# A Fourier filter and a gated layer on one core: the sums and third low parts of the combination move from GpSimd to VectorE

## The chip, the core and the metric

One core of a Trainium2 chip runs the whole program. The metric is the device time of one execution in microseconds (us). Five engines work side by side: TensorE (PE, with its weight loads as PEld), VectorE (DVE), ScalarE (ACT), GpSimd (POOL), and SyncE (SP), which here only issues transfers.

## What is computed

The reference, cut to what matters (numpy; 8 batches of 3008 rows of 256):

```
X = rfft(x, axis=1);  Xr, Xi = X.real, X.imag
Yr = Xr @ w_r - Xi @ w_i + b_r
Yi = Xr @ w_i + Xi @ w_r + b_i
Yr, Yi = soft threshold of each by 0.01
y = irfft(Yr + 1j * Yi, n=3008, axis=1)
h = y @ w_in            # 256 -> 2048
out = (h * cos(h)) @ w_out   # 2048 -> 256
```

All is float32. A float32 product is made on TensorE from two parts of each operand, a rounded high part and the low part that is left, in three matmuls (high by high, low by high, high by low).

## The kernel before

**Two streams.** The main stream is the layer: 8 batches of 6 tiles of 512 rows (the last of 448), and for each tile 16 steps `f`, one per 128 columns of `w_in`: 768 steps. Beside it, while batch `b` goes through the layer, the Fourier filter of batch `b+1` is made. `fourier` (a generator) gives out its work piece by piece, and each step of the layer pulls some of it by written-out costs. A scheduler then sets the order on each engine from its own estimates of time; on the chip each engine takes its instructions in that order and waits for semaphores.

**A step of the layer** (`moe_step`, `second`) is a chain through four engines. TensorE makes `ph` in six matmuls (L939 to L941, 128x512 each); ScalarE rounds `ph` over two pi to whole turns (L949); VectorE subtracts (L950); ScalarE takes the sine (L952); VectorE multiplies by `ph` (L953); ScalarE casts the product to its high part `gh` (L954); then the low part `gl` is formed, by GpSimd (`rest_pool`, L329) where `f` mod 4 is 0 or 2, by VectorE (`rest`, L332) otherwise. TensorE's second product reads `gh` in four matmuls (L921, L922) and `gl` in two (L925). It trails the first product by three steps (`SKEW`), so that the chain has time.

**The combination** (`combine`) belongs to the Fourier filter. For a batch it runs four times (`q` = 0 to 3), for batches 1 to 7: 28 times. It takes the real part `z[:, 0]` and the imaginary part `z[:, 1]` of the spectrum, each in two halves `v`, and forms three operands for the product with the weights: the real part, the imaginary part and their sum. Each is split in high and low:

- first operand: ScalarE casts `Xh` (L602), VectorE subtracts `Xl` (`rest`, L332), for both halves;
- the sum is written in place over the real part (L609), on GpSimd, so it waits for the first operand's low part; beside it ScalarE casts the imaginary part (L610) and VectorE forms its low part (L332);
- third operand: ScalarE casts the sum (L617), GpSimd forms its low part (`rest_pool`, L329).

`wmix` then multiplies the operands by the weights into `pw`: L668 and L669 read high parts, L670 low parts, and the first of its products reads the third operand (the sum). Its results pass through VectorE (L679 to L694) and a `fold` on GpSimd (L707 to L719) into block transposes on VectorE (L724, L725).

Of the kernel before, what the change touches and what calls it, by code (L numbers as in the profile page):

```python
# [19 lines left out]
ALU = mybir.AluOpType  # L20
# [158 lines left out]
def tile_body(ctx: ExitStack, tc, x, w_r, w_i, b_r, b_i, w_in, w_out,  # L179
              c_fq, c_sig, c_f3, c_ff, c_if, c_iw, c_sgn, out):  # L180
    nc = tc.nc
# [139 lines left out]
    def floor():  # L321

        ctx = ExitStack()
        for ins in steps[-2] if len(steps) > 1 else ():
            ctx.enter_context(tc.issue_after(ins.ins))
        return ctx

    def rest_pool(lo, x, hi):
        return nc.gpsimd.tensor_tensor(out=lo, in0=x, in1=hi.bitcast(F32), op=ALU.subtract)  # L329

    def rest(lo, x, hi):
        return nc.vector.tensor_tensor(out=lo, in0=x, in1=hi.bitcast(F32), op=ALU.subtract)  # L332
# [199 lines left out]
    def stage_b(b):  # L532
# [58 lines left out]
        def combine(q):  # L591

            z = Z.pop(q).rearrange("p (v z g m k) -> p g v z m k", v=2, z=2, g=2, m=8)[..., :24]
            xyh = wk.tile([128, 2304], F32R, tag="Xh", name="Xh", bufs=1)
            xyl = wk.tile([128, 2304], F32R, tag="Xl", name="Xl", bufs=1)
            hi, lo = ([m[:, 768 * r:768 * r + 768].rearrange("p (v m z k) -> p v z m k", v=2, m=8, z=2) for r in range(3)]
                      for m in (xyh, xyl))
            X[q] = tuple([[m[:, 768 * r:768 * r + 768].rearrange("p (v c x) -> p c v x", v=2, c=2)[:, c] for c in range(2)]
                          for r in range(3)] for m in (xyh, xyl))
            for v in range(2):  # L600
                with floor():
                    nc.scalar.copy(hi[0][:, v], z[:, 0, v])  # L602
                yield 0.8
                with floor():
                    rest(lo[0][:, v], z[:, 0, v], hi[0][:, v])
                yield 0.9
            for v in range(2):
                with floor():
                    nc.gpsimd.tensor_tensor(out=z[:, 0, v], in0=z[:, 0, v], in1=z[:, 1, v], op=ALU.add)  # L609
                    nc.scalar.copy(hi[1][:, v], z[:, 1, v])  # L610
                yield 0.9
                with floor():
                    rest(lo[1][:, v], z[:, 1, v], hi[1][:, v])
                yield 1.2
            for v in range(2):
                with floor():
                    nc.scalar.copy(hi[2][:, v], z[:, 0, v])  # L617
                yield 0.8
                with floor():
                    rest_pool(lo[2][:, v], z[:, 0, v], hi[2][:, v])  # L620
                yield 0.9

        X, ST = {}, {}
# [187 lines left out]
        def first():  # L811
# [7 lines left out]
            yield from inverse(3)  # L819

        return SimpleNamespace(first=first, load=load, forward=forward, combine=combine, wmix=wmix, inverse=inverse)

    stages = {}
# [289 lines left out]
```

## Time and profile before

| what | value |
|---|---|
| median of 3 runs | 2598.45 us (2598.3 to 2601.07) |
| the profiled execution: its own time | 2597.48 us |
| the profiled execution: span from first to last instruction | 2595.7 us |
| TensorE matmuls busy | 99% of the span |
| VectorE, ScalarE, GpSimd busy | 75%, 63%, 38% |
| mean granted clock of TensorE | 0.997 |

How to read it: the busy share of an engine is an average over the program. Matmul ends are modelled, so a busy row overlaps the next one; what TensorE loses is read from its idle times in the list of waits and in the rows in order of time. A row in order of time gives its start, its length, the engine, the line, what it writes and reads with the shape, how many neighbours it merges, and in brackets the idle time of the engine before it with what ended it.

### The profile page before, as it was taken

The numbers are of one execution on the slowest core, as the hardware profiler recorded it, in microseconds if no ns is written. First come the engines' busy times: TensorE is split into PE (matmuls) and PEld (weight loads), VectorE is DVE, ScalarE is ACT, GpSimd is POOL, SyncE is SP. The second block draws the span as 40 slices with busy tenths as digits, with TensorE's granted clock in tenths as the row PEclk, the third lists the DMA queues.
The fourth block names the chain that finished last, engine by engine and source line by source line (L and its number), as shares of the span: only waits on it lengthen the run. The fifth ranks groups of instructions, "written<-read, shape, count | busy, mean of one in ns | idle before, by whom it ended". The sixth has DMA issues, their size and how long they took to land.

```text
span 2595.7 us, 42932 instructions
## 1 busy us (share of the span) xinstructions
PE 2558.0 (99%) x15961; PEld 2064.4 (80%) x15961; DVE 1938.6 (75%) x3089; ACT 1628.6 (63%) x3003; POOL 977.6 (38%) x946
## 2 busy tenths in 40 slices
PE   9899999999999999999999999999999999999999
PEld 7477778877788778887788877887778888888888
DVE  5887876877778777787777877777776778766665
ACT  5665556665665666666666666666666666666666
POOL 2035452544324453344523454234432333322222
PEclk9999999999999999999999999999999999999999
DMA  7536434354334443254432644235433334210000
GB/s 236 175 107 166 130 110 117 106 143 130 112 87 118 133 132 106 81 151 129 138 88 85 166 130 119 90 101 141 130 101 102 89 106 121 60 49 21 17 25 16
DMA packets 172953, 283.11 MB, mean 109 GB/s; under 512 B 15608, under 2 KB 114200, under 8 KB 169160
## 3 DMA queue, kind: packets, MB, share of 16 engines
q1 hardware_dynamic: 161896, 243.78, 33.5%
q0 software_dynamic: 10112, 35.53, 4.3%
q8 instruction: 126, 2.06, 0.3%
q10 hardware_dynamic: 736, 1.05, 0.1%
q14 instruction: 83, 0.68, 0.1%
HBM read 149.76 MB, written 130.55 MB: 108 GB/s over the span
## 4 chain that ended last, share of the span: by engine, by line
PE 84%; DVE 8%; ACT 3%; DMA 2%; issue 2%; POOL 0%; SPq 0%; DVEq 0%; ACTq 0%; POOLq 0%
PE ph L939 12%; PE po L921 12%; PE ph L940 12%; PE ph L941 11%; PE po L925 11%; PE po L922 11%; PE pw L668 2%; PE pw L669 2%; PE pw L670 2%; DVE u L953 2%; PE pb L381 1%; PE pc L381 1%; DVE u L950 1%; DVE Xl L332 1%; ACT gh L954 1%
## 5 line engine op out<-in xcount | busy, mean ns | idle before, releaser
L329 POOL TENSOR_TENSOR gl<-u,gh 128x512 fp32r<-128x512 f32 (+1 forms) x384 | 501.4, 1306 | 1115.8 <-ACT gh L954 928.4
L952 ACT ACTIVATE u<-u 128x512 f32<-128x512 f32 (+1 forms) x768 | 478.0, 623 | 389.1 <-DVE u L950 388.2
L953 DVE TENSOR_TENSOR u<-ph,u 128x512 f32<-128x512 f32 (+1 forms) x768 | 518.0, 675 | 237.8 <-ACT u L952 226.6
L950 DVE SCALAR_TENSOR_TENSOR u<-ph,u 128x512 f32<-128x512 f32 (+1 forms) x768 | 513.4, 671 | 236.5 <-ACT u L949 235.6
L954 ACT CAST gh<-u 128x512 fp32r<-128x512 f32 (+1 forms) x768 | 467.8, 609 | 250.3 <-DVE u L953 247.9
L921 PE MATMUL po<-gh,wout 128*128 128x512 f32 (+1 forms) x1536 | 600.0, 391 | 15.9 <-ACT gh L954 15.8
L949 ACT ACTIVATE u<-ph 128x512 int32<-128x512 f32 (+1 forms) x768 | 447.6, 586 | 259.2 <-PE ph L941 250.5
L939 PE MATMUL ph<-xTh,win 128*128 128x512 f32 (+1 forms) x1536 | 603.4, 393 | 1.8 <-ACT xTh L901 1.6
L940 PE MATMUL ph<-xTl,win 128*128 128x512 f32 (+1 forms) x1536 | 595.9, 388 | 0.1
L941 PE MATMUL ph<-xTh,win 128*128 128x512 f32 (+1 forms) x1536 | 594.9, 387 | 0.0
L922 PE MATMUL po<-gh,wout 128*128 128x512 f32 (+1 forms) x1536 | 593.8, 387 | 0.0
L925 PE MATMUL po<-gl,wout 128*128 128x512 f32 (+1 forms) x1536 | 476.1, 387 | 0.0
L939 PEld LDWEIGHTS ph<-xTh,win 128*128 128x128 f32 x1536 | 289.3, 188 | 90.6 <-issue 18.4
L332 DVE TENSOR_TENSOR gl<-u,gh 128x512 fp32r<-128x512 f32 (+1 forms) x384 | 297.2, 774 | 79.8 <-ACT gh L954 71.6
L921 PEld LDWEIGHTS po<-gh,wout 128*128 128x128 f32 x1536 | 288.2, 188 | 86.1 <-ACT gh L954 26.2
L925 PEld LDWEIGHTS po<-gl,wout 128*128 128x128 f32 x1536 | 287.2, 188 | 60.1 <-issue 4.9
L941 PEld LDWEIGHTS ph<-xTh,win 128*128 128x128 f32 x1536 | 289.5, 188 | 56.9
L940 PEld LDWEIGHTS ph<-xTl,win 128*128 128x128 f32 x1536 | 289.5, 188 | 51.0 <-DVE xTl L902 0.6
L922 PEld LDWEIGHTS po<-gh,wout 128*128 128x128 f32 x1536 | 288.5, 188 | 50.8
L332 DVE TENSOR_TENSOR Xl<-z,Xh 128x384 fp32r<-128x384 f32 x112 | 108.4, 996 | 11.9 <-ACT Xh L602 8.9
L668 PE MATMUL pw<-Xh,wf 128*128 128x384 f32 x336 | 115.0, 342 | 2.2 <-ACT Xh L617 2.2
L717 POOL TENSOR_TENSOR odd<-st 128x184 f32<-128x184 f32 (+1 forms) x112 | 68.2, 611 | 125.5 <-DVE st L694 117.2
(123 smaller groups left out, 2444.0 us busy)
## 6 DMA issues: line engine op xcount, KB each, us to landing
scrF<-at SPq DMA_DIRECT2D x28, 1024.0 KB
z<-scrF SPq DMA_DIRECT2D x112, 256.0 KB
scrT<-tr SPq DMA_DIRECT2D x56, 512.0 KB
y<-scrT SPq DMA_DIRECT2D x112, 256.0 KB
bt<-scr SPq DMA_DIRECT2D x94, 256.0 KB
scr<-ao SPq DMA_DIRECT2D x84, 256.0 KB
scr<-bo SPq DMA_DIRECT2D x224, 96.0 KB
out_dram<-ob SPq DMA_DIRECT2D x80, 256.0 KB
```

Of the source, the lines that this page charges most:

```text
L329: return nc.gpsimd.tensor_tensor(out=lo, in0=x, in1=hi.bitcast(F32), op=ALU.subtract)
L921: mm(po[e][:, :n], wo[0][:, 0, f, es], gh[:, :n], start=f == 0, stop=False)
L922: mm(po[e][:, :n], wo[0][:, 1, f, es], gh[:, :n], start=False, stop=False)
L925: mm(po[e][:, :n], wo[0][:, 0, f, es], gl[:, :n], start=False, stop=f == NFC - 1)
L939: mm(h, win[:, 0, c, fs], th[:, c, :n], start=c == 0, stop=False)
L940: mm(h, win[:, 0, c, fs], tl[:, c, :n], start=False, stop=False)
L941: ins = mm(h, win[:, 1, c, fs], th[:, c, :n], start=False, stop=c == 1)
L949: nc.scalar.activation(k[:, :n], h, AF.Identity, bias=0.25, scale=1.0 / TWO_PI)
L950: nc.vector.scalar_tensor_tensor(out=u[:, :n], in0=h, scalar=1.0 / TWO_PI, in1=k[:, :n], op0=ALU.mult, op1=ALU.subtract)
L952: nc.scalar.activation(u[:, :n], u[:, :n], AF.Sin, bias=HALF_PI, scale=TWO_PI)
L953: product = nc.vector.tensor_tensor(out=u[:, :n], in0=h, in1=u[:, :n], op=ALU.mult)
L954: step = [nc.scalar.copy(gh[:, :n], u[:, :n])]
```

## The change

In `combine`, the two sums (L609) are formed by VectorE, and so are the two low parts of the third operand (L620, `rest` in place of `rest_pool`). Nothing else in the text of the program differs.

```
             for v in range(2):
                 with floor():
-                    nc.gpsimd.tensor_tensor(out=z[:, 0, v], in0=z[:, 0, v], in1=z[:, 1, v], op=ALU.add)
+                    nc.vector.tensor_tensor(out=z[:, 0, v], in0=z[:, 0, v], in1=z[:, 1, v], op=ALU.add)
                     nc.scalar.copy(hi[1][:, v], z[:, 1, v])
...
                 with floor():
-                    rest_pool(lo[2][:, v], z[:, 0, v], hi[2][:, v])
+                    rest(lo[2][:, v], z[:, 0, v], hi[2][:, v])
                 yield 0.9
```

The order in which the scheduler puts the instructions moves with it. Three places follow; all are of batch 4's filter, made while batch 3 goes through the layer, and the filters of batches 2 to 6 repeat them.

VectorE, `q` = 2 (tile 2 of the layer's batch 3; `u_12170`, `u_12216`, `u_12247` are its steps `f` = 2, 3 and 4; `z_11744` and `Xl_12206` are the combination's). Before:

```order
L953 TENSOR_TENSOR u_12170<-ph_12163,u_12170 128x512
L950 SCALAR_TENSOR_TENSOR u_12216<-ph_12209,u_12216 128x512
L332 TENSOR_TENSOR Xl_12206<-z_11744,Xh_12205 128x2x8x24 x2
L950 SCALAR_TENSOR_TENSOR u_12247<-ph_12240,u_12247 128x512
L953 TENSOR_TENSOR u_12216<-ph_12209,u_12216 128x512
```

and with the change:

```order
L953 TENSOR_TENSOR u_12170<-ph_12163,u_12170 128x512
L609 TENSOR_TENSOR z_11744<-z_11744 128x2x8x24
L950 SCALAR_TENSOR_TENSOR u_12216<-ph_12209,u_12216 128x512
L332 TENSOR_TENSOR Xl_12206<-z_11744,Xh_12205 128x2x8x24 x2
L609 TENSOR_TENSOR z_11744<-z_11744 128x2x8x24
L950 SCALAR_TENSOR_TENSOR u_12247<-ph_12240,u_12247 128x512
L953 TENSOR_TENSOR u_12216<-ph_12209,u_12216 128x512
```

One sum stands ahead of the subtraction of step 3, the other behind the two low parts and ahead of the product of step 3.

VectorE, `q` = 3 (tile 3 of the same batch; `u_12803`, `u_12876`, `u_12902` are its steps 3, 5 and 6). Before:

```order
L332 TENSOR_TENSOR gl_12805<-u_12803,gh_12804 128x512
L332 TENSOR_TENSOR Xl_12828<-z_12402,Xh_12827 128x2x8x24 x3
L953 TENSOR_TENSOR u_12876<-ph_12869,u_12876 128x512
L950 SCALAR_TENSOR_TENSOR u_12902<-ph_12895,u_12902 128x512
L332 TENSOR_TENSOR gl_12878<-u_12876,gh_12877 128x512
```

and with the change:

```order
L332 TENSOR_TENSOR gl_12805<-u_12803,gh_12804 128x512
L332 TENSOR_TENSOR Xl_12828<-z_12402,Xh_12827 128x2x8x24
L609 TENSOR_TENSOR z_12402<-z_12402 128x2x8x24
L332 TENSOR_TENSOR Xl_12828<-z_12402,Xh_12827 128x2x8x24 x2
L953 TENSOR_TENSOR u_12876<-ph_12869,u_12876 128x512
L609 TENSOR_TENSOR z_12402<-z_12402 128x2x8x24
L332 TENSOR_TENSOR Xl_12828<-z_12402,Xh_12827 128x2x8x24
L950 SCALAR_TENSOR_TENSOR u_12902<-ph_12895,u_12902 128x512
L332 TENSOR_TENSOR gl_12878<-u_12876,gh_12877 128x512
```

The product of step 5 now has one sum more ahead of it, and behind it the second sum and one of the third low parts come ahead of step 6.

TensorE at the same place (`gh_12848` and `gl_12849` are of step 4, `gh_12877` of step 5; `pw_12919` is the first product of `wmix`, which reads the combination; `ph_12927` is step 7). Before:

```order
L922 MATMUL po1_12831<-gh_12848,wout_804 128x512
L668 MATMUL pw_12919<-Xh_12827,wf_84 128x384
L669 MATMUL pw_12919<-Xh_12827,wf_84 128x384
L939 MATMUL ph_12927<-xTh_12092,win_85 128x512
L940 MATMUL ph_12927<-xTl_12093,win_85 128x512
```

and with the change:

```order
L922 MATMUL po1_12831<-gh_12848,wout_804 128x512
L925 MATMUL po0_12830<-gl_12849,wout_804 128x512
L925 MATMUL po1_12831<-gl_12849,wout_804 128x512
L921 MATMUL po0_12830<-gh_12877,wout_804 128x512
L922 MATMUL po0_12830<-gh_12877,wout_804 128x512
L921 MATMUL po1_12831<-gh_12877,wout_804 128x512
L922 MATMUL po1_12831<-gh_12877,wout_804 128x512
L668 MATMUL pw_12919<-Xh_12827,wf_84 128x384
L669 MATMUL pw_12919<-Xh_12827,wf_84 128x384
L939 MATMUL ph_12927<-xTh_12092,win_85 128x512
```

The end of step 4 and the four matmuls on `gh` of step 5 now stand ahead of `pw` and of the first products of steps 7 and 8; before, they stood behind them.

## Rows read from the trace of the kernel before

**Rows 1.** The page: the span, and busy time of each engine.

```profile
span 2595.7 us, 42932 instructions
PE 2558.0 (99%) x15961; PEld 2064.4 (80%) x15961; DVE 1938.6 (75%) x3089; ACT 1628.6 (63%) x3003; POOL 977.6 (38%) x946
```

**Rows 2.** Groups by line and shape: count, busy us, mean ns, idle before.

```profile
L332 DVE TENSOR_TENSOR Xl<-z,Xh 128x384 fp32r<-128x384 f32 x112 | 108.4, 996 | 11.9 <-ACT Xh L602 8.9 <-ACT Xh L610 3.0
...
L609 POOL TENSOR_TENSOR z<-z 128x384 f32<-128x384 f32 x56 | 67.7, 1224 | 25.1 <-DVE Xl L332 25.1
L329 POOL TENSOR_TENSOR Xl<-z,Xh 128x384 fp32r<-128x384 f32 x56 | 66.9, 1207 | 23.8 <-ACT Xh L617 23.8
```

**Rows 3.** Waits of TensorE: us in total, times, longest us.

```profile
PE po L921 <- ACT gh L954: 15.8, 13, 2.7
...
PE pw L668 <- ACT Xh L617: 2.2, 5, 0.5
```

**Rows 4.** In order of time, VectorE, GpSimd idle: two low parts in a row, and one.

```profile
1082.64 1.02 DVE L332 TENSOR_TENSOR Xl<-z,Xh 128x384 fp32r<-128x384 f32 x2
...
1194.13 0.55 DVE L332 TENSOR_TENSOR Xl<-z,Xh 128x384 fp32r<-128x384 f32 x1
```

**Rows 5.** In order of time, VectorE, `q` = 2 of batch 4.

```profile
1198.31 0.68 DVE L950 SCALAR_TENSOR_TENSOR u<-ph,u 128x512 f32<-128x512 f32 x1
1199.49 2.71 DVE L332 TENSOR_TENSOR Xl<-z,Xh 128x384 fp32r<-128x384 f32 x2 [0.50 <-ACT Xh L602]
1202.12 0.68 DVE L950 SCALAR_TENSOR_TENSOR u<-ph,u 128x512 f32<-128x512 f32 x1
```

**Rows 6.** In order of time, GpSimd, the same place.

```profile
1199.18 1.29 POOL L329 TENSOR_TENSOR gl<-u,gh 128x512 fp32r<-128x512 f32 x1 [6.30 <-issue]
1200.42 2.65 POOL L609 TENSOR_TENSOR z<-z 128x384 f32<-128x384 f32 x2
```

**Rows 7.** In order of time, TensorE, the same place.

```profile
1204.10 0.50 PE L921 MATMUL po<-gh,wout 128*128 128x512 f32 x1 [1.81 <-ACT gh L954]
```

**Rows 8.** In order of time, VectorE, `q` = 3 of batch 4.

```profile
1264.13 2.32 DVE L332 TENSOR_TENSOR Xl<-z,Xh 128x384 fp32r<-128x384 f32 x3
1266.37 0.68 DVE L953 TENSOR_TENSOR u<-ph,u 128x512 f32<-128x512 f32 x1
```

**Rows 9.** In order of time, GpSimd, the same place.

```profile
1264.81 1.22 POOL L609 TENSOR_TENSOR z<-z 128x384 f32<-128x384 f32 x1 [3.35 <-DVE Xl L332]
1265.99 1.61 POOL L329 TENSOR_TENSOR gl<-u,gh 128x512 fp32r<-128x512 f32 x1
```

**Rows 10.** In order of time, ScalarE, the same place: `gh` of steps 4 and 5.

```profile
1264.33 0.60 ACT L954 CAST gh<-u 128x512 fp32r<-128x512 f32 x1
...
1267.08 0.62 ACT L954 CAST gh<-u 128x512 fp32r<-128x512 f32 x1 [0.50 <-DVE u L953]
```

**Rows 11.** In order of time, TensorE, the same place.

```profile
1265.55 0.40 PE L921 MATMUL po<-gh,wout 128*128 128x512 f32 x1
1265.79 0.39 PE L922 MATMUL po<-gh,wout 128*128 128x512 f32 x1
1266.63 0.44 PE L668 MATMUL pw<-Xh,wf 128*128 128x384 f32 x1 [0.45 <-ACT Xh L617]
```

**Rows 12.** In order of time, `q` = 1 of batch 4: VectorE, GpSimd, TensorE.

```profile
1136.61 0.86 DVE L332 TENSOR_TENSOR gl<-u,gh 128x512 fp32r<-128x512 f32 x1
...
1136.87 2.44 POOL L329 TENSOR_TENSOR Xl<-z,Xh 128x384 fp32r<-128x384 f32 x2
...
1140.21 0.34 PE L670 MATMUL pw<-Xl,wf 128*128 128x384 f32 x1
```

**Rows 13.** In order of time, TensorE, `q` = 2 of batches 1 and 6.

```profile
274.26 0.50 PE L921 MATMUL po<-gh,wout 128*128 128x512 f32 x1 [2.70 <-ACT gh L954]
...
1834.11 0.50 PE L921 MATMUL po<-gh,wout 128*128 128x512 f32 x1 [1.84 <-ACT gh L954]
```

**Rows 14.** A stretch: its length, busy us of PE, PEld, DVE, ACT, POOL; PEclk.

```profile
1834.00:1839.00 5.00, 4.89 (x16) 4.11 (x17) 4.26 (x6) 2.85 (x7) 4.02 (x3) 0.66 0.51 101
```

More of the change, by code (lines that the diff above doesn't have):

```diff
@@ L608, in combine @@
                 with floor():
-                    nc.gpsimd.tensor_tensor(out=z[:, 0, v], in0=z[:, 0, v], in1=z[:, 1, v], op=ALU.add)
+                    nc.vector.tensor_tensor(out=z[:, 0, v], in0=z[:, 0, v], in1=z[:, 1, v], op=ALU.add)
                     nc.scalar.copy(hi[1][:, v], z[:, 1, v])
@@ L619, in combine @@
                 with floor():
-                    rest_pool(lo[2][:, v], z[:, 0, v], hi[2][:, v])
+                    rest(lo[2][:, v], z[:, 0, v], hi[2][:, v])
                 yield 0.9
```

## The prediction

> **What bounds the kernel now.** I read the page first. TensorE is busy for 99% of the span [rows 1], so what the other engines do counts only where TensorE waits for them. VectorE is busy for 75% and GpSimd for 38% [rows 1]; these are averages and say nothing on the moments of waiting. So the list of TensorE's waits came next [rows 3]: 15.8 us in 13 waits for `gh`, the cast that ends the chain of a step, and 2.2 us in 5 waits for the high part of the third operand. Then the rows in order of time around these waits. The reader is to see that they lie at the combination: in the filters of batches 2 to 6, which repeat each other, at `q` = 2 a single wait for `gh` [rows 7], at `q` = 3 a short one for the sum's cast [rows 11]; in batch 1 the longest [rows 13]. At `q` = 0 and `q` = 1 TensorE does not stop. All that the change can give back is therefore some 18 us (15.8 + 2.2), and what follows from a wait in the clock.
>
> Why the waits come can be seen at `q` = 2. VectorE's two low parts at 1199.49 take 2.71 us [rows 5], where the same two take 1.02 with GpSimd idle [rows 4]. Beside them GpSimd runs `gl` and then both sums [rows 6]. VectorE resumes when GpSimd's instruction ends: `gl` ends at 1200.47, the first low part at about 1200.9. So two instructions that both read SBUF on the two engines exclude each other, and one blocked on VectorE costs (2.71 - 1.02)/2 = 0.85 us more. A free one adds 0.47 to a row: 1.02 for two less the 0.55 of one alone [rows 4].
>
> **What the change adds and takes away.** Off GpSimd go 56 sums of 1224 ns and 56 low parts of 1207 ns, 134.6 us [rows 2]. No transfer, no TensorE and no ScalarE instruction is added or removed. VectorE gets 112 instructions; nothing there shows a sum on VectorE, but a low part of the same shape and inputs is the nearest row, so 112 x 0.47 = 52.6 us. What VectorE gets back: the 112 low parts it has now take a mean of 996 ns against 0.55 free [rows 2, 4], 50 us of blocking in all, and the part of it due to the moved instructions ends. But GpSimd keeps half of all `gl`, so the added instructions can be blocked in their turn. On VectorE's total the two nearly cancel, and the time is decided by the order at the few places where TensorE waits. I walk these.
>
> *`q` = 2, batches 2 to 6 (five times).* One sum now stands ahead of step 3's subtraction, which has slack: 1198.31 + 0.47 = 1198.78, still done before the low parts can start at 1199.49 (they wait for ScalarE). The first low part is blocked by `gl` as before (1.32), the second is now free (0.47), the second sum adds 0.47: step 4's subtraction, ahead of step 3's product, starts at 1201.75 and not at 1202.12 [rows 5]. TensorE's wait of 1.81 [rows 7] shrinks by 0.37. Five times: **-1.9 us**. Bounds: nothing blocked, -1.2 each; both blocked, +0.5 each; so -6.0 to +2.5.
>
> *`q` = 3, batches 2 to 6.* Before, GpSimd holds the second sum until 1266.03 and starts step 4's `gl` only at 1265.99 [rows 9], though its `gh` is there at 1264.93 [rows 10]. With the sums gone `gl` starts at about 1265.0, and ends at 1266.3. On VectorE the row is now low part, sum, low part, low part, product: from 1264.13 [rows 8] in steps of 0.47 it would reach the product at 1266.01, but `gl` meets the last two, one is blocked, and the product starts at 1266.86 where it started at 1266.37 [rows 8]. From product to the end of `gh` it is 1.33 (1266.37 to 1267.70 [rows 8, 10]), so `gh` of step 5 is there at 1268.2. This lateness was covered before: `pw` and two first products stood ahead of step 5 on TensorE. In the new order the cover is gone, since step 5 stands ahead of them. TensorE is free at 1265.79 + 0.24 = 1266.03 [rows 11]. Before it resumed at 1266.63, a loss of 0.60. Now it has two matmuls on `gl` (0.48) and then stands until 1268.2: a loss of 1.7, or 1.1 more. Five times: **+5.5 us**. Bounds: nothing blocked, `gh` at 1267.3, +0.25 each; both blocked, +1.9 each; so +1.2 to +9.5.
>
> *The clock.* After the wait of 1.84 us before 1834.11 [rows 13] the granted clock of the next 5 us was 0.66 [rows 14], a mix of the 2.4 GHz level and the 1.2 GHz one; 0.34 x 5 = 1.7 us lost. That wait becomes 1.47 and I take the dip as gone: **-1.7 us** (0 to -1.7); the wait of 1.81 left none. The new loss of 1.7 at `q` = 3, in two pieces, may bring dips: one in five taken, **+1.7 us** (0 to +8.5).
>
> *`q` = 1, batches 2 to 6.* The third low parts stood on GpSimd and ended at 1136.87 + 2.44 = 1139.31, 0.9 before TensorE's first L670 at 1140.21 [rows 12]. Now they follow the `gl` of step 1136.61 on VectorE [rows 12], pushed by two sums (0.94) and up to two blockings (1.7), and take 0.94: 1139.3 to 1141.0, while the new order draws the L670 a little forward. A wait of 0 to 1.7; GpSimd has little to run there, so nearer to zero: 0.3 taken, **+1.5 us** (0 to +8.5).
>
> *`q` = 0, and batches 1 and 7.* At `q` = 0 the sums come behind a product with 0.7 us idle after it and shift nothing that TensorE waits for: 0. In batch 1 the wait of 2.70 [rows 13] keeps its length, I judge: the blockings end, but the order puts step 11's product behind one more subtraction. Batch 7's TensorE waits are none. Together **+1.0 us**, from -5 (both long waits of batch 1 fall under what brings a dip) to +4.
>
> Sum: -1.9 + 5.5 - 1.7 + 1.7 + 1.5 + 1.0 = +6.1 us. The sum stands on the profiled execution, 2597.48 (span 2595.7), which lies 0.97 under the median of 2598.45; carried over to the median, **2604.5 us**.
>
> **Rules that bear on it.** VectorE has no idle time in the waits of rows 5, and the added instructions stand there. The Trainium skill, in "Perfetto Trace Analysis", section Optimizing Scalar/DVE Operations, says that a saturated VectorE may be relieved by other engines, but that moving work between it and GpSimd might not help, as they share a port. By that rule the move gives nothing either way, which is my third case below; the rows agree on the port [rows 4 to 6]. A sum on GpSimd took 1224 ns against 0.55 us for the like row on VectorE [rows 2, 4]. The Trainium skill, in "GPSIMD Engine Reference", section Engine selection, puts elementwise adds on VectorE, with GpSimd about twice as slow; by it the change would be faster, my fourth case.
>
> **The rivals.** I count as no change what lies within 0.2% (5.2 us), about what a measurement of this kernel tells apart: 2593.3 to 2603.6.
> 1. Forecast: the walk above, 2603.7 to 2611. Chance 0.36.
> 2. Worse: each new loss at `q` = 3 brings a dip (5 x 1.7 = 8.5, where 1.7 was counted) or the third low parts at `q` = 1 are late by 1.7 (8.5, where 1.5 was counted): 2604.5 + 6.8 = 2611.3, up to 2618.3 with both. For it: VectorE is full there. Against: a wait of 1.81 left no dip. Chance 0.12.
> 3. The terms cancel: at `q` = 3 `gl` meets no low part, +1.2 and not +5.5, and no dips come, so +6.1 - 4.3 - 1.7 = +0.1: 2598.5. It is decided by whether GpSimd's `gl` starts (1265.0) while VectorE still has low parts to do (1265.07 and 1265.54); the closeness of these numbers is why the chance is as high as 0.36.
> 4. Faster: the blocking by the sums was the cause of most waits. At `q` = 2 nothing is blocked (5 x -1.2 = -6.0), the waits for the sum's cast end (-2.2 [rows 3]), the dip goes (-1.7): -9.9, 2588.5. It decides from the point where `gl` at 1199.18 does not meet the low parts. Against: `gl` there belongs to the layer and stays. Chance 0.16.
>
> That GpSimd still takes part can be left out: no sum and no low part of the combination stands in its new order.
>
> **How the numbers follow.** Slower 0.36 + 0.12 = 0.48, same 0.36, faster 0.16. The range takes the forecast, the third case and most of the second and half of the fourth: 2591 to 2615. The forecast's own range is 2603.7 to 2611.
>
> **What would show it.** Right: TensorE's wait for `gh` at `q` = 2 near 1.4 us; at `q` = 3 a wait of over 1 us for step 5's `gh` that was not there, and no wait of `pw` for the cast; GpSimd 134 us less busy; VectorE's low parts of this shape still bimodal, 0.55 and 1.4. Wrong: no wait at step 5 (the meeting with `gl` misread), or TensorE's waits for `gh` in all under 10 us, or a bill that lies far from the combinations.

## The result, and the profile after

The changed kernel takes **2618.56 us** (median of 4 runs, 2616.08 to 2623.87) against 2598.38 for the kernel before on the same chip: a ratio of 1.0077, 95% interval 1.0065 to 1.0089, or 20 us slower. The prediction was 2604.5, 6.1 us slower, with a range of 2591 to 2615: the direction is right, but the cost is three times as large and the time lies outside the range.

The page of the changed kernel, where [rows 1] stood:

```profile
span 2614.3 us, 42829 instructions
PE 2563.1 (98%) x15961; PEld 2068.1 (79%) x15961; DVE 1962.2 (75%) x3201; ACT 1630.9 (62%) x3003; POOL 841.5 (32%) x834
```

GpSimd is 136 us less busy, VectorE only 24 us more. The group of VectorE's low parts, for [rows 2] (count, busy us, mean ns, idle before), and TensorE's waits, for [rows 3] (us in total, times, longest):

```profile
L332 DVE TENSOR_TENSOR Xl<-z,Xh 128x384 fp32r<-128x384 f32 x168 | 118.0, 727 | 6.7 <-ACT Xh L602 6.4
```

```profile
PE po L921 <- ACT gh L954: 27.3, 20, 4.3
...
PE ph L939 <- DVE u L953: 1.5, 2, 1.0
```

The mean low part fell from 996 to 727 ns, the 56 new ones included. Against 0.55 free that is 30 us of blocking in all (168 x 0.18) where it was 50, so VectorE was indeed freed of part of it. Yet TensorE waits 27.3 us for `gh` where it waited 15.8, and all its waits together grew from 33.0 to 46.4 us (the sums of that view, which lists waits of over 0.15 us). That is 13.4 of the 18.6 us by which the span grew; 5.1 us are clock, below. The wait of `pw` for the sum's cast [rows 3] is gone from the list.

`q` = 3 of batch 4, in order of time, for [rows 8 to 11]: VectorE, GpSimd, ScalarE, TensorE.

```profile
1275.16 0.54 DVE L332 TENSOR_TENSOR Xl<-z,Xh 128x384 fp32r<-128x384 f32 x1
1275.63 0.55 DVE L609 TENSOR_TENSOR z<-z 128x384 f32<-128x384 f32 x1
1276.10 2.11 DVE L332 TENSOR_TENSOR Xl<-z,Xh 128x384 fp32r<-128x384 f32 x2
1278.13 0.68 DVE L953 TENSOR_TENSOR u<-ph,u 128x512 f32<-128x512 f32 x1
1278.73 0.54 DVE L609 TENSOR_TENSOR z<-z 128x384 f32<-128x384 f32 x1
```

```profile
1276.04 1.28 POOL L329 TENSOR_TENSOR gl<-u,gh 128x512 fp32r<-128x512 f32 x1 [4.53 <-ACT gh L954]
```

```profile
1278.84 0.62 ACT L954 CAST gh<-u 128x512 fp32r<-128x512 f32 x1 [1.62 <-DVE u L953]
1279.36 0.51 ACT L617 CAST Xh<-z 128x384 fp32r<-128x384 f32 x1
```

```profile
1274.15 0.50 PE L921 MATMUL po<-gh,wout 128*128 128x512 f32 x1 [1.89 <-ACT gh L954]
...
1279.51 0.50 PE L921 MATMUL po<-gh,wout 128*128 128x512 f32 x1 [0.59 <-ACT gh L954]
```

The reader is to see the queue. VectorE takes a low part, the first sum, two low parts (GpSimd's `gl` starts 0.06 us before them, and the first of them is held until it ends), and only then step 5's product at 1278.13; the second sum stands behind that. So step 5's `gh` ends at 1279.46, and TensorE, which has step 5 next, waits at 1279.51. The wait at 1274.15 is step 3's. It lies ahead of what the change adds at `q` = 3, and was 0.39 long at this place before.

Batch 1, for [rows 13], `q` = 2 and 3:

```profile
277.53 0.50 PE L921 MATMUL po<-gh,wout 128*128 128x512 f32 x1 [3.56 <-ACT gh L954]
...
341.04 0.80 PE L921 MATMUL po<-gh,wout 128*128 128x512 f32 x1 [4.31 <-ACT gh L954]
```

The clock, for [rows 14] (columns as there, the granted clock third from the right). A dip is a stretch like these, in which the granted clock falls to the 1.2 GHz level for a while; the prediction counts 1.7 us for one (0.34 x 5).

```profile
1275.00:1280.00 5.00, 4.41 (x12) 2.89 (x11) 5.00 (x9) 3.00 (x6) 1.28 (x1) 0.66 0.70 161
1592.00:1597.00 5.00, 4.56 (x12) 3.04 (x12) 5.00 (x9) 3.13 (x7) 1.28 (x1) 0.66 0.66 185
1916.00:1921.00 5.00, 4.92 (x16) 4.16 (x17) 2.58 (x5) 2.01 (x5) 1.27 (x1) 0.66 0.39 76
```

In batches 2 to 6 there are three dips, all at `q` = 3, where there was one, at `q` = 2 [rows 14]: 2 x 1.7 = 3.4 us more. The first two start behind the wait of step 3 (1.89 us before 1274.15, 1.92 before 1591.94) and the third behind that of step 5 (1.40 before 1916.08). Like waits left none in batch 2 (1.91 before 640.46, 1.41 before 645.83; granted clock 1.00 from 640 to 650). Batch 1 has 1.7 more (at `q` = 3, 0.58 over the 8 us from 340 against 0.72 over the 6 from 335 before; the one at `q` = 2 is alike).

TensorE's waits for `gh` in us at the places of the prediction, from the rows of each trace (batches 2 to 6 from left to right; "none" and 0 mean none over 0.15); e6, e7 and e17 are experiments below:

| place | before | after | e6: `q` = 3 alone | e7: `q` = 0 to 2 | e17: sums first |
|---|---|---|---|---|---|
| `q` = 2, step 3 | .58 .67 1.81 .74 1.84 | .24 .23 .43 .94 1.42 | .63 .50 .74 .54 .51 | .95 .95 1.45 .95 1.42 | .54 .94 .71 .27 .21 |
| `q` = 3, step 3 | .93 0 .39 .71 .93 | 1.91 .74 1.89 1.92 1.41 | 1.15 .75 1.91 .70 1.91 | 1.12 1.38 .87 1.91 1.14 | .96 1.90 .64 1.91 1.05 |
| `q` = 3, step 5 | none | 1.41 1.40 .59 .74 1.40 | 1.40 1.40 1.40 1.40 .68 | none | none |

### The profile page after: what moved, and what is told of

Same layout as the page of the kernel before. It is cut to its first block, busy times and chain, and to the rows that moved or that the text cites. A ratio compares the mean times of both kernels' runs of the same rounds, so it can differ in the third digit from the quotient of the medians.

```text
span 2614.3 us, 42829 instructions
## 1 busy us (share of the span) xinstructions
PE 2563.1 (98%) x15961; PEld 2068.1 (79%) x15961; DVE 1962.2 (75%) x3201; ACT 1630.9 (62%) x3003; POOL 841.5 (32%) x834
## 3 DMA queue, kind: packets, MB, share of 16 engines
q10 hardware_dynamic: 736, 1.05, 0.1%
## 4 chain that ended last, share of the span: by engine, by line
PE 80%; DVE 9%; DMA 3%; ACT 3%; issue 2%; POOL 2%; SPq 1%; DVEq 0%; ACTq 0%; POOLq 0%
PE ph L939 12%; PE po L921 11%; PE ph L940 11%; PE ph L941 11%; PE po L922 11%; PE po L925 11%; PE pw L668 2%; PE pw L669 2%; PE pw L670 2%; DVE u L953 2%; DVE u L950 2%; DVE Xl L332 1%; PE pc L381 1%; PE pb L381 1%; ACT gh L954 1%
## 5 line engine op out<-in xcount | busy, mean ns | idle before, releaser
L329 POOL TENSOR_TENSOR gl<-u,gh 128x512 fp32r<-128x512 f32 (+1 forms) x384 | 495.2, 1290 | 1333.3 <-ACT gh L954 1104.3
L921 PE MATMUL po<-gh,wout 128*128 128x512 f32 (+1 forms) x1536 | 602.9, 393 | 27.3 <-ACT gh L954 27.3
L332 DVE TENSOR_TENSOR gl<-u,gh 128x512 fp32r<-128x512 f32 (+1 forms) x384 | 283.4, 738 | 71.0 <-ACT gh L954 63.0
L332 DVE TENSOR_TENSOR Xl<-z,Xh 128x384 fp32r<-128x384 f32 x168 | 118.0, 727 | 6.7 <-ACT Xh L602 6.4
L668 PE MATMUL pw<-Xh,wf 128*128 128x384 f32 x336 | 114.3, 340 | 0.3 <-DVE u L953 0.3
L669 PE MATMUL pw<-Xh,wf 128*128 128x384 f32 x336 | 113.8, 339 | 0.0
```

The costliest lines, as they stand in the source:

```text
L921: mm(po[e][:, :n], wo[0][:, 0, f, es], gh[:, :n], start=f == 0, stop=False)
```

## The experiments

The expectations of e1 to e4 weigh three theories of the bill, that is of the 20 us: theory 1 (the order on TensorE at `q` = 3, with VectorE late there), 2 (the number of instructions that VectorE gets) and 3 (the clock). Those from e5 on weigh **A** (VectorE's amount of work around `q` = 2 and 3 is what is paid) and **B** (GpSimd's remaining instructions meet VectorE's at other moments). **C**, formed last, is the place in VectorE's queue. The kernel before ran beside each group of kernels; its medians there were 2598.58 to 2600.83. Each time below is a median, with its ratio to the kernel before in the same group and the 95% interval.

### One half alone: e1 and e2

e1 has the first line of the change's diff, e2 the second.

> Only the sums go to VectorE; the third low parts stay on GpSimd. In this kernel's order step 5's product with `gh` stands ahead of `pw` on TensorE at `q` = 3, as in the change. Theory 1 (the order of TensorE at `q` = 3, and VectorE late there): nearly the whole bill, 2611 to 2619, with a wait of over 1 us at step 5 in batches 2 to 6. Theory 2 (the bill goes by the number of instructions that VectorE gets, each by its own time and by GpSimd's blocking): half of it, 2606 to 2610. Theory 3 (mostly the clock: 10 us more of the span at the 1.2 GHz level, 5 us lost): decided by the number of dips; with those of before, at most 2613.

> Only the third low parts go to VectorE; the sums stay on GpSimd. In this order step 5's product with `gh` stands behind `pw` at `q` = 3, as before the change. Theory 1: little of the bill, 2595 to 2603, no wait for `gh` at step 5. Theory 2: the other half of the bill, 2606 to 2610. Theory 3: by the dips, 2598 to 2604.

Measured: **2626.71** (1.0105 [1.0090, 1.0120]) and **2615.11** (1.0068 [1.0053, 1.0083]). The sums alone cost more than the whole, the low parts alone three quarters of it, and no theory's range holds either time. That is against theory 1 (e2 keeps TensorE's order and pays 15), against halves that add, and more than dips alone could make. In e1, `q` = 3 of batch 4 on VectorE and GpSimd, and batch 2's step 5 on TensorE:

```profile
1280.33 2.91 DVE L332 TENSOR_TENSOR Xl<-z,Xh 128x384 fp32r<-128x384 f32 x2
1283.16 0.68 DVE L953 TENSOR_TENSOR u<-ph,u 128x512 f32<-128x512 f32 x1
```

```profile
1280.27 1.28 POOL L329 TENSOR_TENSOR gl<-u,gh 128x512 fp32r<-128x512 f32 x1 [4.54 <-ACT gh L954]
1281.51 1.31 POOL L329 TENSOR_TENSOR Xl<-z,Xh 128x384 fp32r<-128x384 f32 x1
```

```profile
645.72 0.80 PE L921 MATMUL po<-gh,wout 128*128 128x512 f32 x1 [2.21 <-ACT gh L954]
```

The low part that stayed on GpSimd follows `gl` and blocks a second instruction (2.91 for two where the change has 2.11), and step 5 waits 2.21 where it waited 1.41. So moving the rest off GpSimd does help where the sums have moved. What e2 pays for is not settled: step 5 does not wait there, and its longer waits are spread, among them 7.6 us at `q` = 2 (5.6 before) and 3.2 for GpSimd's `gl`, which the list of before does not have.

### TensorE's order: e3

```
...
-            mm(po[e][:, :n], wo[0][:, 0, f, es], gh[:, :n], start=f == 0, stop=False)
+            with tc.issue_after(mixed[0].ins) if mixed and mixed[1] == 0 else ExitStack():
+                mm(po[e][:, :n], wo[0][:, 0, f, es], gh[:, :n], start=f == 0, stop=False)
```

`mixed` holds the last matmul of `wmix`'s second product at `q` = 3; the second call after it is step 5's.

> The change, with step 5's product with `gh` held behind the second group of `pw` at `q` = 3 (the order before the change); nothing else is edited. Theory 1: the five waits at step 5 (1.1 us each) go and some of the lateness after them: 2609 to 2613. If the waits at step 3 make the larger part of the 3.3 us that each `q` = 3 costs: 2612 to 2616. Theory 2: the wait only moves to `pw`, 2616 to 2620. Theory 3: by the dips, 2613 if those behind `q` = 3 go.

Measured: **2625.39** (1.0101 [1.0082, 1.0121]), worse than the change, and above every range of the text; the sign of theory 2, a wait that moves to `pw`, is there. The second sum on VectorE, its cast and `pw` on TensorE, batch 4:

```profile
1286.66 0.68 DVE L959 TENSOR_TENSOR u<-ph,u 128x512 f32<-128x512 f32 x1
1287.26 0.54 DVE L609 TENSOR_TENSOR z<-z 128x384 f32<-128x384 f32 x1
```

```profile
1287.90 0.51 ACT L617 CAST Xh<-z 128x384 fp32r<-128x384 f32 x1
```

```profile
1288.46 0.45 PE L668 MATMUL pw<-Xh,wf 128*128 128x384 f32 x1 [1.81 <-ACT Xh L617]
```

Step 5 no longer waits, but `pw`, now first, waits 1.81 for the second sum's cast. Before, GpSimd made that sum beside VectorE's low parts [rows 8, 9]; now both stand in one queue. With this order on VectorE the "cover" of the prediction (`pw` ahead of step 5) is lost even where TensorE keeps its order of before.

### The floor: e4

> The sums and the third low parts are formed by no engine: the third operand's high part is cast from the first operand, and TensorE reads the second operand's low part in place of the third's. The time of this kernel is the floor of what any place for the two can give. Theory 1: TensorE's waits at `q` = 2 and 3 nearly go: 2583 to 2592, so that GpSimd's share of before costs 6 to 15 us and VectorE's 26 to 35. Theory 2: the same work costs more on VectorE, by its blocking; before is 5 us above this floor at most: 2593 to 2598.

Measured: **2596.42** (0.9985 [0.9976, 0.9995]). It is in the range of theory 2. With the work left out altogether only some 4 us are gained, so the sums and low parts cost nearly nothing where they were, on GpSimd, and there was little to win by a move. As a floor it is rough: the scheduler's order shifts in this kernel too.

### VectorE's load alone: e5

```
                     rest(lo[1][:, v], z[:, 1, v], hi[1][:, v])
+                    rest(lo[1][:, v], z[:, 1, v], hi[1][:, v])
...
+                    rest(lo[1][:, v], z[:, 1, v], hi[1][:, v])
                     rest_pool(lo[2][:, v], z[:, 0, v], hi[2][:, v])
```

> The kernel before, in which VectorE forms each second low part twice more at the end of the combination and beside the sums' place: 112 more instructions of 0.47 us on VectorE in all, as many as the change adds, while GpSimd keeps its sums and third low parts. TensorE's order at `q` = 3 is that of before. Theory A (VectorE has no idle time around `q` = 2 and 3, so what is added there comes out in TensorE's waits, whoever frees GpSimd): at least the change's own bill, 2614 to 2632. Theory B (the bill comes from GpSimd's remaining instructions, which run at other moments once the moved ones are gone and meet VectorE's): little, 2598 to 2608, since GpSimd's row is untouched.

Measured: **2642.19** (1.0167 [1.0151, 1.0184]), 44 us for 112 instructions, beyond A's own range. The group of low parts, and TensorE's waits:

```profile
L332 DVE TENSOR_TENSOR Xl<-z,Xh 128x384 fp32r<-128x384 f32 x224 | 207.1, 954 | 9.3 <-ACT Xh L602 6.2 <-ACT Xh L610 2.5
```

```profile
PE po L923 <- ACT gh L956: 34.6, 17, 3.2
```

Nothing was relieved and the added ones are blocked like the rest (mean 954 against 996). So VectorE's time in the combination is dear, although VectorE is idle for a quarter of the span. That the change's own 20 us are what is left of such a bill after the relief would fit, but is not shown.

### Where: e6, e7, e8

The change at one `q` or some (`nc.vector if q == 3 else nc.gpsimd`, and so on).

> The change made in the combinations of q = 3 alone; q = 0, 1 and 2 keep the sums and third low parts on GpSimd. Theory A: q = 3 carries most of the bill, about 16.7 us of the 18.6 in the trace of the change: 2608 to 2617, with a wait at step 3 that is no longer than before and one of 1.1 to 1.4 us at step 5. If the lateness is brought in from q = 1 and 2: 2602 to 2608. Theory B: by the meetings at step 5 alone, 2603 to 2607.

> The complement: the change at q = 0, 1 and 2, and q = 3 as before. Theory A as the prediction's steps have it (q = 3 pays): 2596 to 2603. If the lateness comes from q = 1 and 2 (the wait at step 3 of q = 3 grew in the change although that step lies ahead of the added instructions of its own combination): 2605 to 2612, with that wait at 1.4 to 1.9 us. Theory B: 2605 to 2612 too, but with longer rows of VectorE ahead of the waits and not a later start of them.

> The change at q = 2 alone. The prediction's own step for q = 2 is -0.37 us each in batches 2 to 6 and up to 1.7 for the dip at 1834.9: 2594 to 2600. Theory A: the row ahead of the wait is shorter by one blocking and longer by one sum, and two more low parts stand behind it, so TensorE pays at q = 3's step 3: 2600 to 2606. Theory B: 2596 to 2600.

Measured: **2612.75** (1.0053 [1.0038, 1.0068]), **2607.08** (1.0031 [1.0020, 1.0042]), **2602.05** (1.0009 [0.9999, 1.0018]). `q` = 3 carries 14 us, the other three 8.5, of which `q` = 2 no more than some 5: the parts about add to the whole. e6 and e8 lie in A's ranges, e7 in those of B and of lateness brought in. The table shows step 5's wait in e6 alone, as long as in the change. Step 3's at `q` = 3 is longer than before in e6 and in e7 alike, so it cannot be put down to either.

### Less on VectorE: e9 and e10

> The change, with the second operand's low parts left out (TensorE reads the first operand's in their place): VectorE has 112 instructions of 0.47 us fewer than in the change, 56 fewer than before it has low parts, and GpSimd is free of the combination. TensorE's order at q = 3 is that of the change. Theory A (VectorE's own row ahead of TensorE's waits is the bill): as many instructions leave VectorE as the change brought, so the bill goes: 2592 to 2601. Theory B (GpSimd's remaining instructions at other moments): they still meet what VectorE has, and the order stays: 2606 to 2616.

> The kernel before, with the second low parts on GpSimd as well: VectorE gets 112 instructions fewer, GpSimd 112 of 1.2 us more. Theory A: VectorE's row ahead of step 4's gh at q = 2 loses both low parts (2.7 us with the blocking), so the waits of 15.8 us shrink and it may be faster than before: 2586 to 2597. Against it: GpSimd needs 1.2 us for each and holds the sums back, so the third operand's cast comes later and TensorE waits there: 2600 to 2612. Theory B: more work on GpSimd blocks more of VectorE's: 2600 to 2610.

Measured: **2597.61** (0.9988 [0.9978, 0.9998]) and **2603.84** (1.0009 [1.0000, 1.0018]). Both texts miscount: 56 instructions leave VectorE, not 112 (its row on the page goes from 3201 to 3145 instructions in e9, from 3089 to 3033 in e10). In e9 as many instructions have left as half of what came, and yet the whole bill is gone, under TensorE's order of the change at `q` = 3: against B and theory 1, and more than A would have it. What left are the low parts that stand ahead of step 5's product, and step 5 does not wait. In e10 the waits for `gh` fall to 11.4 us, but `pw` waits 7.7 us for the sum's cast (2.2 before): GpSimd is late with the sums, the counter-argument of the text. A's hope for it missed.

### Which steps' `gl` is on GpSimd: e11, e12, e13, e14

e11 and e12: `POOL_GL = (1, 3)` for `(0, 2)`. e13 and e14, in tile 3 only (`on_pool` then stands in place of `f % 4 in POOL_GL`):

```
...
+        on_pool = f == 5 if t == 3 and f in (4, 5) else f % 4 in POOL_GL
...
```

> The kernel before, with GpSimd's half of gl on the odd steps and not on the even ones. The amount of work on each engine is the same; only the places where gl meets VectorE's instructions move. Theory A: the same time within 5 us, 2594 to 2604. If the time hangs on where single instructions meet (the even steps fitted by choice): 2605 to 2620.

> The change, with gl on GpSimd on the odd steps. Theory A: the bill stays, 14 to 24 us over the kernel before with the same odd steps. If the bill belongs to the meeting of step 4's gl with the low parts at q = 3 (an even step, now on VectorE): the two odd kernels lie within 8 us.

Measured: **2605.28** (1.0018 [1.0007, 1.0029]) and **2604.65** (1.0018 [1.0008, 1.0028]). Both are some 5 us above the kernel before, and with `gl` on the odd steps the change costs nothing beyond that. The bill is therefore no fixed price of VectorE's work: A in that form falls. The two are no clean pair, though. In e11 TensorE has the order that the change has at `q` = 3, step 5 ahead of `pw`, and waits there for step 4's `gl` from VectorE (five of these six waits):

```profile
PE po L925 <- DVE gl L332: 7.1, 6, 1.5
```

In e12 TensorE has the order of before, `pw` ahead of step 5. The second theory of e12's text names step 4's `gl`, so it was moved by itself:

> The change; around q = 3 alone (the steps of tile 3) the gl of step 4 goes to VectorE and that of step 5 to GpSimd; step 5's product stays ahead of pw on TensorE. If the meeting of step 4's gl with the low parts is what q = 3 costs (0.85 us of blocking, 5 times, and its dips): 8 to 14 us less than the change, 2604 to 2611, with a wait at step 5 under 0.6 us. Theory A (VectorE's own row, which now has gl's 0.6 us instead of the blocking's 1.1): 2614 to 2618. If TensorE's order is what costs: no change, 2616 to 2620.

> The control of the run before: the same exchange of the gl of steps 4 and 5 at q = 3 in the kernel before. VectorE's third low part is blocked there by the second sum and not by gl, so nothing is to be gained: 2597 to 2606 by every theory.

Measured: **2616.22** (1.0061 [1.0045, 1.0076]) and **2603.65** (1.0010 [1.0000, 1.0020]). In e13 the waits of step 5 for `gh` are gone, and TensorE waits for step 4's `gl` instead, which now stands in VectorE's queue behind the product and the second sum:

```profile
PE po L921 <- ACT gh L954: 18.9, 14, 4.2
PE po L925 <- DVE gl L332: 8.1, 5, 1.6
```

The time is where A's range had it (2614 to 2618). e13 does not settle what the meeting costs: without it step 5's product comes 1.1 us earlier behind step 4's (3.06 us in place of 4.16 in batch 4), but a late `gl` of step 4 has taken the place of the late `gh`. What e12 has, beside TensorE's order of before, is another order of VectorE at `q` = 3 (batch 4, with `pw` on TensorE):

```profile
1272.35 0.53 DVE L332 TENSOR_TENSOR Xl<-z,Xh 128x384 fp32r<-128x384 f32 x1
1272.81 0.54 DVE L609 TENSOR_TENSOR z<-z 128x384 f32<-128x384 f32 x1
1273.27 1.27 DVE L953 TENSOR_TENSOR u<-ph,u 128x512 f32<-128x512 f32 x2
1274.46 0.54 DVE L609 TENSOR_TENSOR z<-z 128x384 f32<-128x384 f32 x1
1274.93 1.01 DVE L332 TENSOR_TENSOR Xl<-z,Xh 128x384 fp32r<-128x384 f32 x2
```

```profile
1276.05 0.45 PE L668 MATMUL pw<-Xh,wf 128*128 128x384 f32 x1
```

There the scheduler put the products of steps 4 and 5 and the second sum ahead of the second operand's low parts. In the change step 5's product and the second sum stand behind them. In e12 neither `pw` nor step 5 waits at `q` = 3 of batches 2 to 6, where e3, with TensorE's order of before and VectorE's of the change, waits 1.81 at `pw`. That VectorE's order is what is paid is theory C.

### Batch 1: e15 and e16

Both choose by `b > 1`; e16 has the odd steps too.

> The change without batch 1: there the sums and third low parts stay on GpSimd. In the trace of the change batch 1 was 4.5 us longer than before, and the prologue 1.3. If that is batch 1's own bill (longer waits at q = 1, 2 and 3 and a dip): 4 to 6 us less than the change, 2612 to 2615. If it only shifts what batch 2 pays: within 2 us of the change.

> The change with gl on the odd steps and without batch 1, the two edits joined. If they add up: 4 to 6 us less than 2604.65, so 2598 to 2601, no faster than the kernel before by what can be measured. If the floor (2596.42 with neither sums nor third low parts formed anywhere) can be reached: 2594 to 2598.

Measured: **2614.52** (1.0052 [1.0037, 1.0067]) and **2611.48** (1.0042 [1.0029, 1.0056]). Batch 1's own bill is 4 us, as expected. e16 missed: it is slower than e12 by 7 us, where it should be faster. Edits that move the schedule do not add up here, and why e16 lost is not settled.

### VectorE's order: e17 and e18

```
             for v in range(2):
                 with floor():
-                    nc.vector.tensor_tensor(out=z[:, 0, v], in0=z[:, 0, v], in1=z[:, 1, v], op=ALU.add)
+                    ins = nc.vector.tensor_tensor(out=z[:, 0, v], in0=z[:, 0, v], in1=z[:, 1, v], op=ALU.add)
                     nc.scalar.copy(hi[1][:, v], z[:, 1, v])
-                yield 0.9
-                with floor():
+            yield 1.8
+            for v in range(2):
+                with floor(), tc.issue_after(ins.ins) if q == 3 else ExitStack():
                     rest(lo[1][:, v], z[:, 1, v], hi[1][:, v])
```

`ins` is the second sum. The low parts are held behind it at `q` = 3 alone, but the loop is split for every `q`, so the two sums are issued together everywhere. e18 adds this to e6.

> The change, with VectorE's order at q = 3 altered and nothing else: both sums stand ahead of the second operand's two low parts (those are held behind the second sum), so that step 5's product comes 2 us earlier in the queue, behind one sum and not behind a blocked and a free low part as well. TensorE's order, with step 5 ahead of pw, stays. Theory C (what is paid at q = 3 is that the product and the second sum wait in one queue behind low parts that are needed later): the waits of 1.4 us at step 5 go, and the dips after them; 2604 to 2611, near the change at q = 0 to 2 alone (2607). Theory A (VectorE's amount of work there): the same amount, only later; the wait returns at the pw products that read the low parts: 2614 to 2620.

> The change at q = 3 alone, with both sums ahead of the second low parts there; at q = 0 to 2 GpSimd keeps its part, in the order in which both sums are issued together. Theory C: q = 3 costs no more than before, where a short wait of pw for the second sum's cast stood: 2594 to 2603. Theory A: as the change at q = 3 alone, 2609 to 2616.

Measured: **2608.05** (1.0035 [1.0022, 1.0049]) and **2608.49** (1.0041 [1.0028, 1.0054]). e17 gives back 10.5 of the change's 20 us, as C said and A did not. VectorE and GpSimd at `q` = 3 of batch 4, and the waits:

```profile
1273.05 0.55 DVE L609 TENSOR_TENSOR z<-z 128x384 f32<-128x384 f32 x1
1273.52 0.68 DVE L954 TENSOR_TENSOR u<-ph,u 128x512 f32<-128x512 f32 x1
1274.12 1.06 DVE L609 TENSOR_TENSOR z<-z 128x384 f32<-128x384 f32 x1
1275.11 1.49 DVE L332 TENSOR_TENSOR Xl<-z,Xh 128x384 fp32r<-128x384 f32 x3
```

```profile
1273.47 1.30 POOL L329 TENSOR_TENSOR gl<-u,gh 128x512 fp32r<-128x512 f32 x1 [4.53 <-PE po L926]
```

```profile
PE po L922 <- ACT gh L955: 16.0, 14, 3.1
PE po L926 <- POOL gl L329: 3.7, 10, 1.0
```

The instructions and engines are the same, and in batches 2 to 6 so is TensorE's order at `q` = 3; there only the product and the second sum come ahead of the low parts. Elsewhere the order moves too, so not all of the 10.5 us is `q` = 3: in the two traces step 5's waits account for 5.5 us, two dips fewer in batches 2 to 6 for 3.4 and shorter waits for `gh` in batch 1 for 2.9, against 2.7 more for `gl`. Of the 2.11 us that stood ahead of the product, 1.09 was blocking by `gl`; e17 takes blocking and low parts away together and does not tell their shares apart. Step 5's wait is gone in all five batches (table), and the waits for `gh` are 16.0 us against 27.3. e18 missed C's range (2594 to 2603) and lies at the edge of A's (2609 to 2616), 4 us under e6. Step 5's waits are gone there too, but all five waits at `q` = 2 are now 1.3 to 1.7 us (0.5 to 0.7 in e6); that the two sums issued together made them so is likely but not shown. No kernel that does all the work is faster than the one before; the two below it, e4 and e9, leave work out.

## Why the prediction was wrong in size

The sum was +6.1 us; the two profiled executions differ by 18.6. The steps that failed are two terms that were far too small, batch 1 and the clock, and a wait for which the sum has no term. Term by term:

- **The place**: right. The largest part of the bill lies at `q` = 3 (14 of 20 us, e6), by the wait for step 5's `gh` that the prediction named, and the `pw` wait is gone.
- **`q` = 2, -1.9**: the five waits fell from 5.64 to 3.26 us, -2.4. The mechanism is right: in batch 4 the row from the low parts to step 4's subtraction is 0.42 shorter, where 0.37 was forecast. That the five sum so near is in part luck, since batch 4's wait alone fell by 1.38 and batch 5's grew by 0.20.
- **`q` = 3, +5.5**: step 5's five waits are 5.54 us in place of 2.2 at `pw`, +3.3; two were hidden in part by a dip. Within its bounds. The mechanism, though, was only half named. The walk saw the loss of cover on TensorE and one blocked low part. e3 shows that the cover does not help with VectorE's order of the change, since the second sum is as late, and e17 shows that step 5's wait goes when the blocked and the free low part no longer stand ahead of the product.
- **The failed step: "I judge" in batch 1, +1.0.** Its waits went from 6.33 (0, 2.70, 2.55, 1.08 at `q` = 1, 2, 3 and one later) to 9.62 us (0.91, 3.56, 4.31, 0.84), +3.3, and its dips +1.7: 5.0, five times the term. e15, without the change in batch 1, is 4 us faster than the change. The judgement that the wait of 2.70 "keeps its length" had no row behind it.
- **The failed step: the clock, -1.7 + 1.7.** Measured +5.1, of which the 1.7 in batch 1 are the same as above. The dip at `q` = 2 went, as forecast, but three of five places `q` = 3 have one, not one in five, and two of the three follow step 3's wait, which the walk did not have. The bound of +8.5 held it.
- **`q` = 1, +1.5**: no wait for a low part is in TensorE's list after, so 0.
- **What has no step**: step 3's wait at `q` = 3, 2.96 us in five before and 7.87 after, +4.9. The walk took every place from the phases of before, as if what is won or lost at one place did not shift how early TensorE comes to the next. What sets this wait is not settled: it is some 6.4 in e6, e7 and e17, about 5 in e4, 3.7 in e14, and 6.6 in e9, which is no slower than the kernel before. The profiled execution before, at 2597.48, lies low among the runs of that kernel (2594.73 to 2605.89), and with 2.96 may flatter it. So the +4.9 is read from one pair of traces and need not be a price of the change.
- TensorE's waits for `u` (1.5) and `gl` (1.0) were not foreseen either. The terms make -2.4 + 3.3 + 4.9 + 3.3 + 5.1 + 1.5 + 1.0 = 16.7 of the 18.6 us; the rest lies in small waits elsewhere. One reading was loose: VectorE "has no idle time" in rows 5, but it has 0.50 us there, ahead of the low parts.
- **The rivals.** The "worse" case was half right: dips came, in three batches and not at every new loss, but nothing was late at `q` = 1. That its upper end, 2618.3, lies next to the measured time is luck, since batch 1 and step 3's wait are not in it. "The terms cancel" fell: `gl` did meet a low part. "Faster" fell too: the waits for the sum's cast and the dip at `q` = 2 went as it says, but `gl` still meets the first low part there, and it does not see `q` = 3 and batch 1. By "Perfetto Trace Analysis" of the Trainium skill, section Optimizing Scalar/DVE Operations, a move between the two engines might not help; e4 agrees that there was little to gain. By "GPSIMD Engine Reference" of the Trainium skill, section Engine selection, adds belong on VectorE. For the single instruction the rows agree, 0.55 us (1275.63 above) against 1.22 on GpSimd [rows 2], and the kernel is 20 us slower all the same.

## What to carry to other kernels

An instruction moved to a faster engine joins that engine's one queue. Here what it cost was set by what stands behind it there, more than by its length or by the engine's busy share; two critical things that ran side by side are now late one after the other. After such a move, look in the order for products and casts that stand behind work needed later, and put those first: in e17 the kernel with that order got back half of the bill. The other half is not explained by it. And in a schedule made by estimates, an edit shifts the phases of places it does not touch: judge it by several alignments (e11, e12), not by one.

## What the runs showed of the hardware

- Blocking went by the instruction's inputs. In e17 the product at 1273.52 reads `ph`, which lies in PSUM, beside `gl` of GpSimd (1273.47 to 1274.77) and takes its usual 0.68; the sum behind it, with both inputs in SBUF, takes 1.06 for 0.55. None of the 768 products of that trace took over 0.70. The Trainium skill, in "SBUF — State Buffer", section Who interferes with whom, says that a VectorE instruction with at most one input in SBUF, outside its two-port modes, does not contend with GpSimd, and that one with two does with a GpSimd instruction that reads SBUF; the rows agree.
- A blocking can cost more than the 0.85 us of the prediction: where `gl` started 0.06 us ahead (1276.04 against 1276.10), two low parts took 2.11 where two free ones take 1.02 [rows 4], 1.09 more.
- A dip pays part of the next wait. At 1274.15 TensorE waited 1.89; the granted clock of the stretch behind was 0.66, TensorE came later to step 5, and waited 0.59 there where batches without a dip between wait 1.40 (table). Batch 5 shows the same, 0.74 behind the dip at 1592, and batch 6 of e6 0.68. So for a forecast a wait and a dip just ahead of it are not to be added in full.
